# Output stores regrouped: one transfer takes both column halves of a token group, or a whole block of 384 KB, from all 128 partitions

## The chip, the core and the metric

The kernel runs on one core of a Trainium2 chip. TensorE (PE) multiplies, VectorE (DVE), ScalarE (ACT) and GpSimd (POOL) move and convert data, and SyncE (SP) issues nearly all transfers. A transfer is one instruction on SP or ACT; its bytes are moved by the core's 16 DMA engines. On-chip memory has 128 partitions, and a tile is addressed as partitions x elements. The metric is the device time of one execution in microseconds (us), lower is better.

## What is computed

Sigmoid attention, followed by a token-mixing layer on its result. Shapes: q, k and v are (8, 12, 448, 64), the result is (8, 448, 768), all float32.

```python
scores = scale * q @ k.T - log(S)            # per batch and head, S = 448
attn   = 1 / (1 + exp(-scores)) @ v
x      = attn, heads side by side            # (8, 448, 768)
W_tok  = (x @ w_q) @ (x @ w_k).T / sqrt(64)  # (8, 448, 448)
out    = relu(W_tok @ x) @ w_out             # (8, 448, 768)
```

## The kernel before

The work goes by 24 "quads": one batch and four heads each, three quads to a batch. For every quad, q, k and v are loaded (448 KB each) into one of six float32 load buffers (`ld`), cast to bf16, mostly by POOL, transposed, multiplied to scores, passed through the sigmoid on ACT and multiplied with v. When a batch has its three quads, the mixing layer runs for it (`mlp_wqk`, `mlp_wkn`, `mlp_tmp`, `mlp_mix`). When a pair of batches `w` (0 to 3) is done, its last product with `w_out` runs in output chunks, between the matmuls of later quads. The order of all of this is written out by hand as a string of letters (`PLAN`); letter `O` is a step of an output chunk and `D` issues one queued store (`flush(1)`). Instructions stand on each engine in the order in which the program issues them.

There are two kinds of output chunk:

- For the pairs 0 and 1, `out_chunk` makes a block `o` of 128 partitions x 768 columns: 128 tokens of all columns, written in two column halves. A token is `p * 7 + i`, with `p` from 0 to 63 and `i` from 0 to 6 (`NI` = 7), so a block holds two values of `i`, the first on partitions 0 to 63 and the second on 64 to 127. Seven blocks make a pair; in the fourth the two `i` lie in different batches. Its store (L652) is two transfers, one for each half of the partitions, 192 KB each.
- For the pairs 2 and 3, `out_pair` makes a tile of 128 partitions x 2 x 384. Partitions 0 to 63 hold the columns 0 to 383, partitions 64 to 127 the columns 384 to 767; the index in the middle, `y`, tells token index `k` from `k + 4`. Its store (L608) is two transfers of 192 KB, one for each half of the partitions (each column half `x`). There are 12 such tiles, 24 transfers, one of them (the very last) on ACT's queue. The last tiles (`late`) use the load buffers, which are free by then; all others come from a pool of five `o` buffers. The seventh token index is stored apart (L613, L559, L561); the change does not touch that.

`store` is put on a list, and issued at a later `D`, at the latest when an `o` buffer is needed again. The transfers of the SP queue share eight completion semaphores in turn: a transfer is issued only when the eighth before it has landed, and an instruction that waits holds what stands behind it on SP. The loads of the quads are issued on the same queue, between the stores, each as soon as the cast that read the buffer before is done. A transfer's destination and source are access patterns: lists of (step, count), outermost first. The shape that the order shows for a store is that of its destination: `64x768` is 64 token rows of 768 columns, and its source begins with the 64 partitions.

Of the kernel before, what the change touches and what calls it, by code (L numbers as in the profile page):

```python
# [17 lines left out]
def kernel(  # L18
# [12 lines left out]
    nc = tc.nc  # L31
# [5 lines left out]
    NI, NP = 7, 64  # L37
# [4 lines left out]
    HALF = (slice(0, 64), slice(64, 128))  # L42
# [34 lines left out]
    def bank2():  # L77
        n = int(given.pop(0))
        assert not held & {2 * n, 2 * n + 1}
        held.update({2 * n, 2 * n + 1})  # L80
        return n, pairs[n], pairs16[n]

    def bank1():
        b = "abcdefgh".index(given.pop(0))
        assert b not in held
        held.add(b)
        return "abcdefgh"[b], pairs[b // 2][:, b % 2], pairs16[b // 2][:, b % 2]

    def release(fb):
        gone = {2 * fb, 2 * fb + 1} if isinstance(fb, int) else {"abcdefgh".index(fb)}  # L90
        assert gone <= held
        held.difference_update(gone)
# [16 lines left out]
    def ld_next():  # L109
        nld[0] += 1  # L110
        return lds[(nld[0] - 1) % 6]
# [8 lines left out]
    def mm(*args, **kw):  # L120
        products.append(nc.tensor.matmul(*args, **kw))  # L121
# [399 lines left out]
    def flush(n=None):  # L521

        for _, f in stores[:n]:
            f()
        del stores[:n]

    def o_tile(shape):

        while stores and stores[0][0] <= o_tiles[0] - 5:
            flush(1)  # L530
        o_tiles[0] += 1
        return p_o.tile(shape, F32, tag="o", name="o")

    def slot(half, b):

        return b // 2 + (0 if b % 2 == half else NC)

    def middle(w, us, k, part, fb, ps):

        x = part // 2  # L540
        for c in range(part % 2 * NC // 2, (part % 2 + 1) * NC // 2):
            for u in us:
                st = mxs[w].rearrange("p (c u s) -> p c u s", u=2, s=S)[:, c, u, 3 * NP : 4 * NP]
                mm(
                    ps[HALF[u], x, 0:NB], st, wout16[:, c, x * NB : (x + 1) * NB],
                    start=(c == 0), stop=(c == NC - 1),
                )
        if part % 2:
            if not x:
                ot[0] = ld_next()[:, 0:D]  # L550
            o = ot[0][:, x * NB : (x + 1) * NB]
            half = NB // 2
            for y in range(2):
                cols = slice(y * half, (y + 1) * half)
                COPY["vs"[y]](out=o[:, cols], in_=ps[:, x, cols])
            rows = out[2 * w : 2 * w + 2].rearrange("u (p i) d -> (u p) i d", i=NI)[:, NI // 2, x * NB : (x + 1) * NB]
            if x:
                for y in range(2):
                    (nc.sync, nc.scalar)[y].dma_start(out=rows[HALF[y]], in_=o[HALF[y]])  # L559
            else:  # L560
                nc.sync.dma_start(out=rows, in_=o)  # L561
        if part < 3:
            opened.append((w, us, k, part + 1, fb, ps))
        else:
            release(fb)

    def out_pair(act, tail):

        if opened:
            w, us, k, part, fb, ps = opened.pop()  # L570
        else:
            w, us, k = chunks.pop(0)
            part = 0
            fb, ps, _ = bank2()
        if len(us) == 2 and w == MIXED:
            middle(w, us, k, part, fb, ps)
            return
        mx = mxs[w].rearrange("p (b s) -> p b s", b=12)
        at = S // 2 - 32 if len(us) == 2 else k * NP + (32 + S // 2 if us[0] else 0)
        for b in range(3 * part, 3 * part + 3):  # L580
            for y in range(2):
                st = mx[HALF[y], b, at : at + NP]
                if w == MIXED:
                    j = (b - b % 2) * S + us[0] * S + (b % 2) * 4 * NP + k * NP
                    st = mxs[w][HALF[y], j : j + NP]
                for x in range(2):
                    mm(
                        ps[HALF[x], y, 0:NB], st, wout16[HALF[y], slot(y, b), x * NB : (x + 1) * NB],
                        start=(b == 0), stop=(b == 11),
                    )  # L590
        if part < 3:
            opened.append((w, us, k, part + 1, fb, ps))
            return
        late = len(cast) == len(ORDER) + 2
        ends = w == NU // 2 - 1 and us[-1] and len(chunks) < 2
        o = ld_next()[:, 0:D].rearrange("p (b x) -> p b x", b=2) if late else o_tile([P, 2, NB])
        if ends:
            for y in range(2):
                COPY["vs"[y]](out=o[:, y], in_=ps[:, y, 0:NB])
        else:  # L600
            COPY["s" if act else "v"](out=o, in_=ps[:, :, 0:NB])
        release(fb)

        def store():
            for x in range(2):
                cols = slice(x * NB, (x + 1) * NB)
                if len(us) == 1:
                    (nc.scalar if ends and x else nc.sync).dma_start(  # L608
                        out=out[2 * w + us[0]].rearrange("(p i) d -> p i d", i=NI)[:, k : k + 5 : 4, cols], in_=o[HALF[x]],
                    )  # L610
                    continue
                for u in us:
                    nc.sync.dma_start(  # L613
                        out=out[2 * w + u].rearrange("(r n i) d -> i n r d", r=2, i=NI)[NI // 2, :, :, cols],
                        in_=o[64 * x + 32 * u : 64 * x + 32 * u + 32],
                    )

        stores.append((o_tiles[0] - 1, store))
        if tail or late:
            flush()  # L620

    def out_chunk(act, tail):

        if opened:
            w, m, nb, fb, ps = opened.pop()
            part = 1
        else:
            w, m, nb = chunks.pop(0)
            if nb < 0:
                nb = 0  # L630
                chunks.insert(0, (w, m, 1))
            fb, ps, _ = bank1()
            part = 0
        if nb == 0 and not part:
            ot[0] = o_tile([P, D])
        o = ot[0]
        ps = ps if part else ps[:, 0:NB]
        for c in range(part * NC // 2, (part + 1) * NC // 2):
            mm(
                ps, mxs[w][:, 2 * S * c + m * P : 2 * S * c + (m + 1) * P],  # L640
                wout16[:, c, nb * NB : (nb + 1) * NB], start=(c == 0), stop=(c == NC - 1),
            )
        if not part:
            opened.append((w, m, nb, fb, ps))
            return
        COPY["s" if act else "v"](out=o[:, nb * NB : (nb + 1) * NB], in_=ps)  # L646
        release(fb)

        def store():
            for y in range(2):  # L650
                b, i = divmod(2 * m + y, NI)
                nc.sync.dma_start(out=out[2 * w + b].rearrange("(p i) d -> p i d", i=NI)[:, i], in_=o[HALF[y]])  # L652

        if nb:
            stores.append((o_tiles[0] - 1, store))
# [23 lines left out]
    def cols(r):  # L679
        return slice(r.start * HD, r.stop * HD)  # L680
# [8 lines left out]
        out=ident, in_=ident, compare_op=ALU.not_equal, fill=1.0, base=0,  # L689
# [93 lines left out]
    for t16, t32, r, e in (  # L783
# [3 lines left out]
            out=t16[:, r].rearrange("p i b d -> p b i d"),  # L787
            in_=t32[:, :, cols(r)].rearrange("p b (i d) -> p b i d", d=HD),
# [3 lines left out]
    def tr_part(nm, t16, r, e, tiled=False):  # L792
# [19 lines left out]
        out=k016[:, K3].rearrange("p i b d -> p b i d"), in_=k0[:, :, cols(K3)].rearrange("p b (i d) -> p b i d", d=HD),  # L812
# [10 lines left out]
    for t in PLAN:  # L823
# [17 lines left out]
        c = done[kind]  # L841
# [4 lines left out]
        elif kind == "P":  # L846
            n, i = divmod(c, NI)
# [29 lines left out]
        elif kind == "C":  # L877
            for y in range(2):
                nc.sync.dma_start(
                    out=wout16[HALF[y], NC + 2 * c : NC + 2 * c + 2, :], in_=wout16[HALF[1 - y], 2 * c : 2 * c + 2, :],  # L880
# [5 lines left out]
        elif kind == "M":  # L886
            u, x = divmod(c, NC // 2)
# [42 lines left out]
```

## Time and profile before

| | us |
|---|---|
| median of 3 runs (184.32 to 186.18) | 185.74 |
| the profiled execution | 185.85 |
| its span, from the first to the last instruction | 184.1 |
| what lies around the span in that execution | 1.75 |

The page gives the busy time of each engine, the span in 40 slices, the traffic of the DMA queues, the chain of waits that ended last, and the costliest groups of instructions. A group's line has its source line, engine, operation, what it writes and reads, the count, and durations. The share of the DMA engines is a mean over all 16; a share slightly over 1 comes from packets that overlap on an engine. "To landing" is the time from the issue of a transfer until its last completion signal.

### The profile page before, as it was taken

What the parts mean: (1) busy time and instruction counts of PE and PEld (TensorE: products, weight loads), DVE (VectorE), ACT (ScalarE), POOL (GpSimd) and SP (SyncE); (2) the same over time, 40 slices, a digit from 0 to 9 for tenths busy, and PEclk for the clock granted to TensorE, in tenths of its full rate; (3) what the DMA queues carried; (4) which work ended last, traced back from release to release, by engine and by line L of the source; (5) the groups of instructions that cost most, each with busy time, mean ns of one, the idle gap of its engine ahead of it and who ended that gap; (6) DMA issues with size and microseconds to landing.
All of it is one profiled execution on the core that took longest, in us unless ns stands there. A gap on an engine that the chain in (4) does not pass through costs nothing.

```text
span 184.1 us, 8404 instructions
## 1 busy us (share of the span) xinstructions
PE 171.2 (93%) x3618; PEld 112.3 (61%) x3618; DVE 134.0 (73%) x205; ACT 159.9 (87%) x207; POOL 117.0 (64%) x156
## 2 busy tenths in 40 slices
PE   7987778799999999999999999999999999999990
PEld 7544434454564655565656556456778898888970
DVE  2445679988999898988848877689785894694310
ACT  4699998999999999998998999999989979974330
POOL 1445696999799996799999937999999400000000
PEclk9999999999999999999999999999999999999998
DMA  5999999968999768999979998998992343432686
GB/s 176 370 382 283 305 356 333 394 244 267 400 395 390 226 215 272 353 270 366 338 199 309 313 335 271 325 391 286 303 313 65 90 111 90 109 90 66 148 223 172
DMA packets 24261, 48.51 MB, mean 264 GB/s; under 512 B 3872, under 2 KB 16416, under 8 KB 24224
## 3 DMA queue, kind: packets, MB, share of 16 engines
q1 hardware_dynamic: 24000, 47.69, 79.3%
q8 instruction: 28, 0.46, 1.0%
q10 hardware_dynamic: 224, 0.30, 0.6%
q14 instruction: 9, 0.07, 0.1%
HBM read 35.78 MB, written 11.01 MB: 254 GB/s over the span
## 4 chain that ended last, share of the span: by engine, by line
PE 80%; DVE 5%; ACT 5%; issue 3%; POOL 2%; DMA 2%; SPq 0%; ACTq 0%; POOLq 0%
PE banks L121 76%; PE banks L124 4%; ACT at L331 4%; DMA ld<-in_moe_w_k_dram 2%; DVE xt L355 1%; POOL wqk L754 1%; DVE qk L251 1%; POOL qk L211 1%; DVE qk L264 1%; DVE mx L469 1%; POOL v L221 0%; DVE k L221 0%; DVE xn L384 0%; DVE wqk L429 0%; ACT qk L801 0%
## 5 line engine op out<-in xcount | busy, mean ns | idle before, releaser
L331 ACT ACTIVATE at<-banks 128x896 bf16<-128x896 f32 x168 | 141.6, 940 | 6.6 <-PE banks L121 6.1
L121 PE MATMUL banks<-wout,mx 64*64 64x384 bf16 (+2 forms) x816 | 66.2, 324 | 0.7 <-issue 0.6
L121 PE MATMUL banks<-qk 64*64 64x448 bf16 x672 | 60.8, 358 | 4.2 <-ACT at L331 2.7
L121 PEld LDWEIGHTS <-mx 64*64 64x64 bf16 (+2 forms) x816 | 39.5, 105 | 17.5 <-issue 7.1
L211 POOL CAST qk<-ld 128x896 bf16<-128x896 f32 x38 | 44.6, 1193 | 8.4 <-issue 7.2
L121 PE MATMUL banks<-at,v 64*64 64x448 bf16 x672 | 46.7, 350 | 1.5 <-POOL v L221 0.8
L121 PEld LDWEIGHTS <-qk 64*64 64x64 bf16 x672 | 26.6, 105 | 24.8 <-issue 18.0
L355 DVE CAST xt<-banks 128x896 bf16<-128x896 f32 x23 | 25.0, 1086 | 7.6 <-PE banks L121 5.8
L121 PEld LDWEIGHTS <-v 64*64 64x64 bf16 x672 | 23.3, 106 | 7.5 <-issue 1.5
L469 DVE TENSOR_SCALAR mx<-banks 128x896 bf16<-128x896 f32 (+1 forms) x21 | 19.9, 955 | 5.0 <-PE banks L121 4.2
L221 POOL CAST v<-ld 128x896 bf16<-128x896 f32 x22 | 20.3, 930 | 1.2 <-DMA ld<-in_v_dram 0.6
L271 DVE STREAM_TRANSPOSE qk<-qk 128x448 f32<-128x448 f32 x26 | 16.0, 629 | 0.1
L251 DVE STREAM_TRANSPOSE qk<-qk 32x448 f32<-32x448 f32 x24 | 15.3, 636 | 0.6
L384 DVE COPY xn<-banks 128x896 bf16<-128x896 bf16 x21 | 13.1, 624 | 3.6 <-PE banks L124 2.6
L170 POOL COPY qk<-qk 32x448 uint32<-32x448 uint32 x26 | 14.4, 554 | 1.6
L173 POOL COPY qk<-swap 32x448 uint32<-32x448 uint32 x26 | 14.4, 554 | 1.5
L121 PE MATMUL banks<-xt,wqk 64*64 64x448 bf16 (+1 forms) x84 | 13.8, 353 | 0.2 <-ACT at L331 0.2
L646 DVE COPY o<-banks 128x384 f32<-128x384 f32 x17 | 9.4, 553 | 3.4 <-PE banks L121 3.0
L124 PEld LDWEIGHTS <-xt 64*64 64x64 bf16 (+1 forms) x588 | 9.8, 108 | 3.1 <-issue 1.6
L124 PE MATMUL banks<-ident,xt 64*64 64x64 bf16 (+1 forms) x588 | 10.4, 194 | 0.2
L121 PE MATMUL banks<-wqk,tmp 64*64 64x448 bf16 (+3 forms) x72 | 8.7, 291 | 0.0
L121 PE MATMUL banks<-wq,tmp 64*64 64x448 bf16 (+2 forms) x72 | 8.4, 292 | 0.0
(67 smaller groups left out, 136.1 us busy)
## 6 DMA issues: line engine op xcount, KB each, us to landing
ld<-in_q_dram SPq DMA_DIRECT2D x24, 448.0 KB, 6.1
ld<-in_v_dram SPq DMA_DIRECT2D x24, 448.0 KB, 5.9
ld<-in_k_dram SPq DMA_DIRECT2D x23, 448.0 KB, 5.9
out_dram<-o SPq DMA_DIRECT2D x38, 192.0 KB, 4.9
out_dram<-ld SPq DMA_DIRECT2D x14, 192.0 KB, 3.0
ld<-in_moe_w_out_dram SPq DMA_DIRECT2D x6, 384.0 KB, 5.3
wout<-wout SPq DMA_DIRECT2D x6, 192.0 KB, 5.7
out_dram<-o SPq DMA_DIRECT2D x4, 96.0 KB, 1.9
```

Of the source, the lines that this page charges most:

```text
L121: products.append(nc.tensor.matmul(*args, **kw))
L124: products.append(nc.tensor.transpose(*args, **kw))
L170: eng.tensor_copy(out=w[lo, 1], in_=w[hi, 0])
L173: eng.tensor_copy(out=w[hi, 0], in_=z[lo])
L211: COPY[e](out=f[:, :, "qk".index(nm)].rearrange("p e i d y -> p e y i d"), in_=ld.pop((nm, n)).rearrange("p (y i e d) -> p e y i d", y=2, ...
L221: COPY[e](out=t16.rearrange("p i b d -> p b i d"), in_=ld.pop((nm, n)).rearrange("p b (i d) -> p b i d", i=NI),)
L251: nc.vector.transpose(out=qk[n][other : other + 32, h].rearrange("p t i n -> p (t i n)").bitcast(F32), in_=w[own : own + 32, 1 - h],)
L271: nc.vector.transpose(out=qk[n][:, t].rearrange("p t i n -> p (t i n)").bitcast(F32), in_=w)
L331: nc.scalar.activation(dst, src, ACTF.Sigmoid, bias=attn_bias, scale=attn_scale)
L355: COPY[eng](out=xt(u, j), in_=ps)
L384: COPY[eng](out=xn, in_=ps)
L469: nc.vector.tensor_scalar(dst, ps, moe_scale, 0.0, ALU.mult, ALU.max)
```

## The change

The two `store` functions address their transfers in another way. The number of bytes, the tiles, the arithmetic and the places at which `store` is called stay as they are.

- In `out_pair` there are still two transfers of 192 KB to a tile, but each takes one `y` (one token index) from all 128 partitions, with both column halves. The destination is written as column half, token, column: counts 2, 64, 384.
- In `out_chunk` one transfer of 384 KB takes the whole block of 128 partitions. The destination is token index, token, column: counts 2, 64, 768. The fourth block of each pair, whose two token indices lie in different batches, keeps its two transfers.

```diff
         def store():
+            if len(us) == 1:
+                for y in range(2):
+                    (nc.scalar if ends and y else nc.sync).dma_start(
+                        out=out[2 * w + us[0]].rearrange("(p i) (x c) -> i x p c", i=NI, x=2)[k + 4 * y], in_=o[:, y],
+                    )
+                return
             for x in range(2):
                 cols = slice(x * NB, (x + 1) * NB)
-                if len(us) == 1:
-                    (nc.scalar if ends and x else nc.sync).dma_start(
-                        out=out[2 * w + us[0]].rearrange("(p i) d -> p i d", i=NI)[:, k : k + 5 : 4, cols], in_=o[HALF[x]],
-                    )
-                    continue
                 for u in us:
...
         def store():
+            b, i = divmod(2 * m, NI)
+            if i + 1 < NI:
+                nc.sync.dma_start(out=out[2 * w + b].rearrange("(p i) d -> i p d", i=NI)[i : i + 2], in_=o)
+                return
             for y in range(2):
                 b, i = divmod(2 * m + y, NI)
                 nc.sync.dma_start(out=out[2 * w + b].rearrange("(p i) d -> p i d", i=NI)[:, i], in_=o[HALF[y]])
```

On SP, in the middle of the program, block stores of the pair 0 stand between the loads of later quads. `ld_100` to `ld_105` are the six load buffers; a row's shape is that of its destination.

```order
-L652 DMA out_dram<-o 64x768 x2
+L653 DMA out_dram<-o 2x64x768
 L189 DMA ld_102<-in_q_dram 128x896
 L197 DMA ld_103<-in_v_dram 128x2x448
 L197 DMA ld_104<-in_v_dram 128x2x448
-L652 DMA out_dram<-o 64x768 x6
+L653 DMA out_dram<-o 2x64x768 x3
 L197 DMA ld_105<-in_v_dram 128x2x448
 L189 DMA ld_100<-in_k_dram 128x896
 L189 DMA ld_101<-in_k_dram 128x896
-L652 DMA out_dram<-o 64x768 x2
+L653 DMA out_dram<-o 2x64x768
```

Two transfers became one at each place, and no load changed its place. The outermost count of the destination was 64 and is 2; that of the source was 64 partitions and is 128.

On SP, at the end of the program, the last tiles are stored. Before:

```order
L608 DMA out_dram<-ld_105 64x2x384 x2
L608 DMA out_dram<-ld_100 64x2x384 x2
L608 DMA out_dram<-ld_101 64x2x384
L561 DMA out_dram<-ld_102 128x384
L559 DMA out_dram<-ld_102 64x384
```

And in the changed program:

```order
L607 DMA out_dram<-ld_105 2x64x384 x2
L607 DMA out_dram<-ld_100 2x64x384 x2
L607 DMA out_dram<-ld_101 2x64x384
L561 DMA out_dram<-ld_102 128x384
L559 DMA out_dram<-ld_102 64x384
```

Number and place are the same; the outermost count of the destination went from 64 to 2 here too. On the other engines nothing moved.

## The prediction

> **What bounds the kernel now.** I read the page first: the busy times, the slices, the traffic and the chain of waits.
>
> ```profile
> span 184.1 us, 8404 instructions
> PE 171.2 (93%) x3618; PEld 112.3 (61%) x3618; DVE 134.0 (73%) x205; ACT 159.9 (87%) x207; POOL 117.0 (64%) x156
> DMA  5999999968999768999979998998992343432686
> DMA packets 24261, 48.51 MB, mean 264 GB/s; under 512 B 3872, under 2 KB 16416, under 8 KB 24224
> PE 80%; DVE 5%; ACT 5%; issue 3%; POOL 2%; DMA 2%; SPq 0%; ACTq 0%; POOLq 0%
> ```
>
> PE holds 80% of the chain, transfers 2%. But the DMA digits stand at 9 for three quarters of the span: the 16 engines have little room, and what slows one of them is felt. Then the stretches (columns: window and length, busy us of PE, PEld, DVE, ACT, POOL, the granted clock, the DMA share, GB/s):
>
> ```profile
> 46.50:50.50 4.00, 4.00 (x69) 2.36 (x70) 3.85 (x8) 4.00 (x7) 3.15 (x4) 1.00 1.04 404
> 70.00:135.00 65.00, 65.00 (x1188) 38.39 (x1188) 52.96 (x80) 62.22 (x82) 54.78 (x73) 1.00 0.94 311
> 106.60:108.40 1.80, 1.80 (x36) 0.86 (x32) 1.17 (x2) 1.80 (x4) 0.82 (x2) 1.00 1.00 373
> 161.00:178.00 17.00, 16.64 (x480) 15.11 (x472) 8.28 (x17) 8.32 (x16) 0.00 (x0) 1.00 0.51 122
> 176.00:180.00 4.00, 3.66 (x64) 2.49 (x56) 1.21 (x3) 1.32 (x3) 0.00 (x0) 1.00 0.92 225
> 181.00:182.00 1.00, 0.00 (x0) 0.00 (x0) 0.00 (x0) 0.00 (x0) 0.00 (x0) 1.00 0.88 280
> ```
>
> From 70 to 135 us, where the block stores run between the loads, PE is busy 65.00 of 65.00 us and the DMA engines 0.94 of the time. A full queue moves 404 GB/s (46.5 to 50.5), that is 404/16 = 25.3 GB/s for one engine.
>
> All transfers of the program, by the list of issues (count, KB each, median us to landing):
>
> ```profile
> ld<-in_q_dram SPq DMA_DIRECT2D x24, 448.0 KB, 6.1
> ld<-in_v_dram SPq DMA_DIRECT2D x24, 448.0 KB, 5.9
> ld<-in_k_dram SPq DMA_DIRECT2D x23, 448.0 KB, 5.9
> out_dram<-o SPq DMA_DIRECT2D x38, 192.0 KB, 4.9
> out_dram<-ld SPq DMA_DIRECT2D x14, 192.0 KB, 3.0
> ld<-in_moe_w_out_dram SPq DMA_DIRECT2D x6, 384.0 KB, 5.3
> wout<-wout SPq DMA_DIRECT2D x6, 192.0 KB, 5.7
> out_dram<-o SPq DMA_DIRECT2D x4, 96.0 KB, 1.9
> ld<-in_k_dram SPq DMA_DIRECT2D x1, 256.0 KB, 4.2
> ld<-in_k_dram SPq DMA_DIRECT2D x1, 192.0 KB, 3.3
> ld<-in_moe_w_q_dram SPq DMA_DIRECT2D x1, 192.0 KB, 3.8
> ld<-in_moe_w_k_dram SPq DMA_DIRECT2D x1, 192.0 KB, 5.1
> out_dram<-ld ACTq DMA_DIRECT2D x1, 192.0 KB, 3.8
> out_dram<-ld SPq DMA_DIRECT2D x1, 96.0 KB, 2.6
> out_dram<-ld ACTq DMA_DIRECT2D x1, 96.0 KB, 2.7
> ```
>
> The counts add up to 146. The page has 3872 packets under 512 B. The two loads of w_q and w_k move rows of 64 floats, 256 B: 2 x 192 KB / 256 B = 1536 packets. The other 2336 are 146 x 16: every transfer ends with 16 small packets. I read them as one completion from each of 16 engines, so before the change each transfer is dealt over all 16.
>
> **The change, step by step.** What decides is over how many engines a store is dealt. In the program before, every destination and source begins with a count of 128, 64 or 32, as the shapes of the order show, and 16 goes into each of them. The changed stores begin with 128 on the source side and with 2 on the destination side. If the dealing goes by the outermost counts, which the rows before cannot show but never contradict, a share must be a whole part of both, and 2 shares are the most: two engines carry the store, each 64 rows, and 14 carry nothing. I take this as the likeliest case.
>
> The Trainium skill, "DMA: Bandwidth & Descriptors", section "Why a DMA increments its semaphore by 16 and not by 1", states it as a rule: the engine count is the largest number up to 16 that divides the slowest dimension above 1 of both patterns, and on SP's and ACT's queues the lowest-numbered engines are taken. The trace agrees as far as its 146 x 16 packets go; no run here has a count below 16. By that rule the sum is the one below, with the same two engines each time.
>
> The work of one of these two engines, from the first changed store on. The counts of the loads behind it, and of the stores:
>
> ```profile
> L189 SPq DMA_DIRECT2D ld<-in_k_dram x9: 327/333/1437, 76.3 to 127.4; - x9
> L189 SPq DMA_DIRECT2D ld<-in_q_dram x9: 328/333/1087, 77.3 to 129.4; - x9
> L197 SPq DMA_DIRECT2D ld<-in_v_dram x10: 378/382/1023, 81.2 to 128.2; - x10
> L652 SPq DMA_DIRECT2D out_dram<-o x28: 467/588/1382, 70.0 to 133.9; - x28
> DMA to landing us min/median/max: 4.6/4.9/5.5
> ```
>
> (The last line is of the first six L652 stores alone.)
>
> - Blocks: 28 stores were 14 blocks; 12 become one transfer of 393,216 B, half of it on each engine: 12 x 196,608 = 2.36 MB. At 25.3 GB/s one takes 7.8 us, where two half stores took 2 x 192 KB at 404 GB/s = 1.0 us.
> - Tiles: 24 transfers of 196,608 B, half each: 24 x 98,304 = 2.36 MB; 3.9 us for one, before 0.5.
> - What is dealt over 16 as before: 28 loads x 28,672 B = 0.80 MB; two blocks left as four stores x 12,288 B = 0.05; six wout copies x 12,288 = 0.07; the small stores, 4 x 6,144 and 24,576 = 0.05. Together 0.97 MB.
>
> The sum is 5.69 MB, at 25.3 GB/s 225 us. It begins where the queue ahead of the first block store is done: issued at 70.0, landed up to 5.5 us later, less its own 0.5: 75.0. All of it follows in the engine's order, so the last store lands at 75 + 225 = 300 us. Before, the last one (issued at 180.4, landed 2.6 later, 183.0) left 1.1 us to the end of the span. Span: 301. Around it lie 185.85 - 184.1 = 1.75 us, so 303 us, against a profiled 185.85 and a median of 185.74.
>
> Does this engine ever run empty? That would lengthen the sum. Up to the last load (129.4) it carries loads that the program issues as soon as a buffer is free, and up to 23 us of blocks ahead of them (x3 in the order). A load dealt over 16 lands only with its slowest share, so POOL's casts, and PE behind them, wait. Behind the last load stand 3 x 7.8 + 24 x 3.9 = 117 us of stores, while the kernel before needed 184.1 - 129.4 = 55 us from that issue to its end. So computation gets ahead, waits for `o` and load buffers that stores have yet to leave, and keeps the queue full. SP waits for the eighth transfer before; the loads queued behind that wait are late, but eight transfers in flight keep the engine fed. I add nothing.
>
> SP has 12 transfers fewer, 12 x 0.588 = 7.1 us of issuing; SPq is 0% of the chain, so it is worth nothing. What the change ends, two engines at a time reading one half of the partitions, shows in stores at 225/0.92/16 = 15.3 GB/s per busy engine (176 to 180); this goes in any case, and is inside the rate.
>
> The rate is the unknown. No row shows a store on two engines. At the slow end stands the one late store from 128 partitions, alone on the queue at 181 to 182 us: 280/0.88/16 = 19.9 GB/s, or 286 us, end 364. A stretch of block stores in a full queue (106.6 to 108.4) has 373/16 = 23.3: 244 us, end 322. At the quick end no row goes above 25.3, but there all 16 share what lies behind them; if two alone ran 10% faster: 205 us, end 283. I take 25.3, as these two queues are never empty.
>
> **Rivals.** *The stores stay dealt over 16 engines* (by tokens, or by the source's 128 partitions). For it: bytes and packets stay the same, and 16 goes into 64 and 128. Against: the destination's outermost count is 2. This case ends on the other side, not slower. It decides if the count of 2 is merged away or passed over. Then the price is what waits for these stores: PE has no gap from 70 to 135; in the chain SPq has 0%; among those who waited for stores stands a single line.
>
> ```profile
>   ACT ld L555: 1.1, 1
> ```
>
> So 0 to 1.1 us come out: 184.7 to 185.9. The Trainium skill, same page, "Rules for kernel authors", says that two transfers to disjoint partition halves gain nothing and one of 128 partitions is to be used; no run here shows that yet, and by it this case would be the one.
>
> *Two engines, but other ones each time.* Then the work is even in sum, and no engine collects 225 us. A load behind a group of blocks still waits up to 7.8 - 1.0 = 6.8 us for its slowest share. On SP five groups of blocks stand ahead of loads, 5 x 6.8: 0 to 34 us, less what the buffers cover; the last store adds 3.9 - 0.5 = 3.4. That gives 189 to 223 us; I take 197, since six load buffers lie ahead of the casts. Against it: nothing in a full queue asks for turns, and the transfers before needed none.
>
> **How the numbers follow.** Two fixed engines: 0.84. Dealt over 16: 0.10. Changing pairs: 0.04. Something else, slower: 0.02. The likeliest gives 303 us. From its rates come 283 to 364; I open the lower end to 280. About one part in twenty of the first case may lie outside, so that the range holds 0.8. The other cases are left out of it. Within 1% (1.9 us) is about what a measurement of this kernel can tell from no change. The 16-engine case gives at most 0.6%, so it counts as the same, 0.07, and 0.03 of it as faster, should freed transfers help somewhere that the chain does not show. Slower: 0.84 + 0.04 + 0.02 = 0.90.
>
> **What would show it.** Packets under 512 B: 1536 + 98 x 16 + 36 x 2 = 3176 if the 36 changed transfers have two completions each; 1536 + 134 x 16 = 3680 if they have 16. The DMA digits of the last 80 us at 1 (two of 16 engines), with 2 x 25.3 = 51 GB/s. PE's slices with gaps from 80 us on, and its busy time near 171 as before. Chain: DMA in the first place, with stores. SP's waits for landings, which are small now, in tens of us. A transfer count right and a rate wrong would show as 3176 packets with another GB/s at the end. The forecast falls altogether if the small packets are 3680, or if PE stays at 93%.

## The result: 304.68 us, and the profile after

| | before | changed |
|---|---|---|
| median of 6 runs, us | 186.38 (184.32 to 187.05) | 304.68 (303.27 to 304.78) |
| ratio | | 1.635, 95% interval 1.627 to 1.644 |
| span of the profiled execution, us | 184.1 | 302.9 |
| packets under 512 B | 3872 | 3176 |

The page of the changed kernel: the busy times, three rows of the 40 slices (each now 7.6 us), the traffic, and the chain of waits by engine and by line.

```profile
span 302.9 us, 8385 instructions
PE 187.1 (62%) x3618; PEld 118.8 (39%) x3618; DVE 133.9 (44%) x205; ACT 161.4 (53%) x207; POOL 117.3 (39%) x156
PE   8878899999994079908588596686699400000000
DMA  7989979976328698113394931111131111111111
GB/s 234 388 253 388 388 228 375 355 250 202 98 95 261 215 271 283 54 52 118 147 274 142 316 115 54 54 54 50 52 101 54 50 50 50 50 50 50 62 72 48
DMA packets 23565, 48.51 MB, mean 160 GB/s; under 512 B 3176, under 2 KB 15720, under 8 KB 23528
DMA 47%; PE 22%; ACT 9%; SPq 3%; DVE 3%; POOL 3%; issue 2%; DVEq 0%; ACTq 0%; POOLq 0%
DMA out_dram<-o 30%; PE banks L121 21%; DMA out_dram<-ld 10%; ACT at L331 8%; DMA ld<-in_k_dram 6%; SPq L607 3%; PE banks L124 2%; POOL qk L211 2%; DVE o L601 1%; DVE mx L469 1%; POOL qk L173 0%; POOL qk L170 0%; DVE qk L271 0%; DVE xt L355 0%; POOL v L221 0%
```

Read it from the right. In the last eight slices PE does nothing; the DMA digit is 1, and the traffic 48 to 72 GB/s, mostly 50. The chain went from 80% PE to 47% DMA, two kinds of stores ahead of all loads. The bytes are the same, 48.51 MB. The small packets are 1536 + 98 x 16 + 36 x 2 = 3176, to the packet, as it must be if each of the 36 changed transfers ends with two completions, where all others have 16. One of the 36 can be seen nearly by itself. ACT's queue (`q10`) carries just two transfers, a changed one and the store of 96 KB, in 192 packets of data. Its packets (count, MB, share of the engines), before and changed:

```profile
q10 hardware_dynamic: 224, 0.30, 0.6%
q10 hardware_dynamic: 210, 0.29, 0.3%
```

That is 192 + 16 + 16 before, and 192 + 16 + 2 now.

Four windows of the changed kernel in which its stores stand nearly alone on the queue (the last two columns are the DMA share and GB/s):

```profile
75.50:78.00 2.50, 2.50 (x46) 1.53 (x44) 2.38 (x5) 2.44 (x4) 1.16 (x3) 1.00 0.13 53
180.00:210.00 30.00, 20.69 (x438) 16.23 (x434) 11.88 (x16) 16.40 (x20) 9.09 (x14) 0.85 0.14 53
240.00:285.00 45.00, 0.00 (x0) 0.00 (x0) 1.27 (x3) 1.02 (x3) 0.00 (x0) 0.52 0.14 52
255.00:268.00 13.00, 0.00 (x0) 0.00 (x0) 0.71 (x2) 0.00 (x0) 0.00 (x0) 0.50 0.13 50
```

In the first, two changed blocks are under way. The second still holds the ends of some loads, and the third the small store on ACT's queue, issued at 280.6 us and dealt over all 16. In the last there are the changed stores alone: a share of 0.13 over 16 engines is 2.1 engines, two that are always busy, and 50 GB/s over two is 25 GB/s each. Before, one of 16 engines in a full queue moved 404/16 = 25.3. So an engine works as fast as ever; 14 are left out.

How this reaches PE is seen where loads stand behind the first blocks. POOL of the changed kernel, 84 to 101 us, in order of time (start, length, what; in brackets the idle time ahead and what ended it):

```profile
84.14 0.93 POOL L221 CAST v<-ld 128x896 bf16<-128x896 f32 x1
100.97 2.26 POOL L211 CAST qk<-ld 128x896 bf16<-128x896 f32 x2 [15.90 <-DMA ld<-in_k_dram]
```

The load of k is dealt over 16 engines, but two of its shares stand behind three blocks, 3 x 7.8 us on those engines, the first of which begins at 75 us. It lands when they do; POOL waits 15.9 us for it, and PE's slices of 91 to 106 us show 4 and 0. Some of the large waits, over the whole changed kernel (engine and line, waited for whom, us in total, times, longest):

```profile
ACT at L331 <- PE banks L121: 53.2, 33, 13.0
POOL v L221 <- DMA ld<-in_v_dram: 26.9, 5, 21.8
DVE o L601 <- DMA out_dram<-o: 17.8, 5, 6.4
POOL qk L211 <- DMA ld<-in_k_dram: 16.6, 3, 15.9
DVE o L647 <- DMA out_dram<-o: 13.7, 3, 7.6
```

Late loads and output buffers that have not been emptied hold up computation. Even so it is done long before the stores: the window 240 to 285 has no matmul at all.

### The profile page after: what moved, and what is told of

It is laid out like the page before. It is cut to its first block, busy times and chain, and to the rows that moved or that the text cites. A ratio compares the mean times of both kernels' runs of the same rounds, so it can differ in the third digit from the quotient of the medians.

```text
span 302.9 us, 8385 instructions
## 1 busy us (share of the span) xinstructions
PE 187.1 (62%) x3618; PEld 118.8 (39%) x3618; DVE 133.9 (44%) x205; ACT 161.4 (53%) x207; POOL 117.3 (39%) x156
## 2 busy tenths in 40 slices
DMA packets 23565, 48.51 MB, mean 160 GB/s; under 512 B 3176, under 2 KB 15720, under 8 KB 23528
## 4 chain that ended last, share of the span: by engine, by line
DMA 47%; PE 22%; ACT 9%; SPq 3%; DVE 3%; POOL 3%; issue 2%; DVEq 0%; ACTq 0%; POOLq 0%
DMA out_dram<-o 30%; PE banks L121 21%; DMA out_dram<-ld 10%; ACT at L331 8%; DMA ld<-in_k_dram 6%; SPq L607 3%; PE banks L124 2%; POOL qk L211 2%; DVE o L601 1%; DVE mx L469 1%; POOL qk L173 0%; POOL qk L170 0%; DVE qk L271 0%; DVE xt L355 0%; POOL v L221 0%
## 5 line engine op out<-in xcount | busy, mean ns | idle before, releaser
L121 PE MATMUL banks<-qk 64*64 64x448 bf16 x672 | 65.1, 380 | 37.6 <-DVE xt L355 13.6
L121 PE MATMUL banks<-wout,mx 64*64 64x384 bf16 (+2 forms) x816 | 72.8, 356 | 7.5 <-DVE xt L355 4.0
L121 PEld LDWEIGHTS <-mx 64*64 64x64 bf16 (+2 forms) x816 | 42.0, 114 | 28.5 <-issue 17.1
L121 PEld LDWEIGHTS <-qk 64*64 64x64 bf16 x672 | 27.4, 110 | 61.8 <-issue 54.7
L121 PE MATMUL banks<-at,v 64*64 64x448 bf16 x672 | 49.5, 365 | 0.6 <-ACT at L331 0.3
L121 PEld LDWEIGHTS <-v 64*64 64x64 bf16 x672 | 24.5, 111 | 7.2 <-issue 1.3
L271 DVE STREAM_TRANSPOSE qk<-qk 128x448 f32<-128x448 f32 x26 | 16.0, 630 | 22.4 <-POOL qk L173 22.3
L251 DVE STREAM_TRANSPOSE qk<-qk 32x448 f32<-32x448 f32 x24 | 15.3, 636 | 0.6
L601 DVE COPY o<-banks 128x768 f32<-128x768 f32 x6 | 5.7, 957 | 18.1 <-DMA out_dram<-o 17.8
L124 PEld LDWEIGHTS <-xt 64*64 64x64 bf16 (+1 forms) x588 | 10.5, 112 | 3.3 <-issue 1.8
L647 ACT COPY o<-banks 128x384 f32<-128x384 f32 x11 | 5.4, 491 | 10.1 <-DMA out_dram<-o 9.5
```

The costliest lines, as they stand in the source:

```text
L124: products.append(nc.tensor.transpose(*args, **kw))
L251: nc.vector.transpose(out=qk[n][other : other + 32, h].rearrange("p t i n -> p (t i n)").bitcast(F32), in_=w[own : own + 32, 1 - h],)
L271: nc.vector.transpose(out=qk[n][:, t].rearrange("p t i n -> p (t i n)").bitcast(F32), in_=w)
```

## The experiments

The theory is that of the prediction: a transfer is dealt by the outermost counts of its two patterns, so a count of 2 leaves two engines, and the price is what these two have to move one after the other. Its rivals say that the price lies in the store itself: in reading 128 partitions, in the size of 384 KB, or in the two places of memory to which one store goes.

**even16: the same stores, to 128 rows in one even step.** Two batches of a pair lie 64 x 7 tokens apart, so that row `p` of both forms one run of 128 rows, 7 tokens from one to the next.

```diff
-                        out=out[2 * w + us[0]].rearrange("(p i) (x c) -> i x p c", i=NI, x=2)[k + 4 * y], in_=o[:, y],
+                        out=out[2 * w : 2 * w + 2].rearrange("u (p i) (x c) -> (u p) i x c", i=NI, x=2)[:, k + 4 * y, us[0]], in_=o[:, y],
...
-                nc.sync.dma_start(out=out[2 * w + b].rearrange("(p i) d -> i p d", i=NI)[i : i + 2], in_=o)
+                nc.sync.dma_start(out=out[2 * w : 2 * w + 2].rearrange("u (p i) d -> (u p) i d", i=NI)[:, m], in_=o)
```

> Same transfers as the changed kernel, from all 128 partitions and of the same sizes, but each store goes to 128 output rows of one even step (token rows of two batches), so that its destination begins with a count of 128, not 2. Which rows of the output a block lands in is changed; all bytes are stored once. Dealing by the outermost counts: 16 engines again, 3680 packets under 512 B, 184.5 to 187 us, no slower than before; at most 1.1 us is gained. If one large store from 128 partitions, or the merging, were what costs: it stays near 300 us.

Measured: 185.28 us (median of 12), beside a before of 186.22; ratio 0.996, interval 0.993 to 0.999. The stores read 128 partitions, the blocks are 384 KB, and nothing is lost. The rivals of size and of partitions fall.

**rows2, rows4, rows8: the same rows in 2, 4 and 8 runs.** To both destinations of even16 a split of the 128 rows is added, for rows4:

```diff
-...[:, k + 4 * y, us[0]], in_=o[:, y],
+...[:, k + 4 * y, us[0]].rearrange("(n h) c -> h n c", h=4), in_=o[:, y],
...
-...[:, m], in_=o)
+...[:, m].rearrange("(n h) d -> h n d", h=4), in_=o)
```

Each run has every fourth row.

> The same 128 rows as in even16, but written as 2 runs of 64 (every second row), so that the destination begins with a count of 2; the rows within a block are permuted. Dealing by the outermost counts: two engines, 3176 small packets, 300 to 307 us, as the changed kernel. If where the rows lie in memory (the two token indices, the two column halves) were what costs, it is as fast as even16.

> As rows2 with 4 runs of 32: the destination begins with 4. Dealing by the outermost counts: four engines, 1536 + 98 x 16 + 36 x 4 = 3248 small packets. Each of the four then has 2.36 + 0.97 = 3.33 MB behind 75 us, 132 us at 25.3 GB/s: 75 + 132 + 2.9 = 210 us if it never runs empty, less where computation is the bound; I expect 200 to 212. If a first count below 16 always meant the same slow path, it is near 300; if it cost nothing of its own, 186.

> As rows2 with 8 runs of 16: the destination begins with 8. Dealing by the outermost counts: eight engines, 3392 small packets; 1.18 + 0.97 = 2.15 MB on each of them, 85 us, so their queue would be done at 160 us and no longer sets the end: 185 to 190 us. A cost for each changed store that does not fall with the engine count would show as more.

Measured, one execution each: 304.59, 214.38 and 190.59 us. The traffic line of their pages, of even16, rows2, rows4 and rows8 in turn:

```profile
DMA packets 24069, 48.51 MB, mean 265 GB/s; under 512 B 3680, under 2 KB 16224, under 8 KB 24032
```

```profile
DMA packets 23565, 48.51 MB, mean 160 GB/s; under 512 B 3176, under 2 KB 15720, under 8 KB 23528
```

```profile
DMA packets 23637, 48.51 MB, mean 228 GB/s; under 512 B 3248, under 2 KB 15792, under 8 KB 23600
```

```profile
DMA packets 23781, 48.51 MB, mean 257 GB/s; under 512 B 3392, under 2 KB 15936, under 8 KB 23744
```

All four counts are those expected: 16, 2, 4 and 8 completions for each of the 36 stores. (On ACT's queue, with its one changed store, the packets are 224, 210, 212 and 216.) The output rows within a block's set are the same in all four, in another order, so the place in memory is not the cause either. rows2 repeats the median of the changed kernel within 0.1 us. rows4 is 2 us above the range that I gave, at four engines, and rows8 half a microsecond above its own. Two windows of rows4, from 190 us to 210 us, nearly without matmuls, and from 75 to 135 us:

```profile
190.00:210.00 20.00, 1.10 (x14) 0.53 (x10) 0.71 (x2) 0.54 (x2) 0.00 (x0) 0.66 0.32 115
75.00:135.00 60.00, 51.49 (x816) 28.12 (x815) 38.94 (x59) 48.14 (x64) 38.12 (x50) 0.94 0.78 244
```

At the end the stores set the time, 0.32 x 16 = 5.1 engines' worth of share for four engines and the last small stores. In the middle PE is busy 51.5 of 60.0 us. I had bounded the time by the four engines' queue alone (210 us); it came out 4 us later. Counted in the trace's packets, fewer than four are in flight for only 0.5 us between 75 and 210 us, so no empty queue is seen. The first packet of a changed block starts at 74.1 us and the last of all ends at 211.3: 3.33 MB in 137 us is 24.3 GB/s for one engine, where I had taken 25.3, and that is about the 4 us. rows8 is 4.4 us above its before, 186.22; its page shows one wait of 3.1 us for a store (ACT, L601), and the rest stays open.

**blocks_only and pairs_only: half of the change each.** The one keeps `out_chunk`'s new store and has `out_pair`'s old one, the other the reverse. Against the changed kernel:

```diff
# blocks_only: out_pair as before
-            if len(us) == 1:
-                for y in range(2):
...
# pairs_only: out_chunk as before
-            b, i = divmod(2 * m, NI)
-            if i + 1 < NI:
...
```

> Only the whole-block stores of out_chunk are changed (12 transfers of 384 KB); out_pair's stores are as before. Two engines for these 12: 2.36 MB on each beside the loads of the time from 70 to 135 us, so casts and PE wait for loads that land late. A queue account from the issue times of before gives some 42 us of delay to computation, and the tail of stores dealt over 16 hides nothing: 222 to 238 us. 3872 - 12 x 16 - 12 x 14 = 3512 small packets. If the blocks cost nothing because loads are ahead: 186.

> Only out_pair's stores are changed (24 transfers of 192 KB); whole blocks are stored as before. All but a few of their loads are done by then, so nothing is late but the stores: 24 x 3.9 = 93 us behind the first one, whose queue is free at 139 us: 139 + 93 + 2.9 = 235 us, 228 to 240. 3872 - 24 x 14 = 3536 small packets. PE's last work stays behind by the buffers that stores free late.

Measured: 238.84 and 237.86 us, beside a before of 186.56. The excesses, 52 and 51 us, add up to 104; the whole change costs 304.68 - 186.38 = 118. That the whole costs more than its halves fits a queue in which the tiles' stores stand behind blocks that are themselves late; no run tests it. pairs_only came out 2.9 us above the 235 computed, within its range: there no load is behind the stores, and the sum is only the queue. The page's slices of pairs_only, PE and DMA:

```profile
PE   7987889999999999999999999999993000000000
DMA  6989997999579999999997921151111111111120
```

PE runs full until its end, as before, and nine slices of 5.9 us follow with stores on two engines. blocks_only was just above its range. Its queue is not the end; its loads are late, and when PE was starved its granted clock went down. The window 75 to 180 us of blocks_only (the clock is the third number from the right):

```profile
75.00:180.00 105.00, 73.35 (x1188) 42.77 (x1190) 50.53 (x78) 61.03 (x79) 53.01 (x71) 0.84 0.55 176
```

And the window of the kernel before in which it does as many matmuls, from 75 us on too:

```profile
75.00:138.50 63.50, 63.27 (x1188) 38.10 (x1183) 51.31 (x78) 60.26 (x80) 54.77 (x74) 1.00 0.94 309
```

The 1188 matmuls are busy 10 us longer in blocks_only. My account had no term for these 10 us, which are about what is missing between its middle, 230, and 238.84; no run shows the clock's part by itself.

**half2: half-partition stores, with a count of 2.** The kernel before, its 28 block stores as they are, from 64 partitions and 192 KB each; only the 64 rows are written in two runs of 32.

```diff
-                nc.sync.dma_start(out=out[2 * w + b].rearrange("(p i) d -> p i d", i=NI)[:, i], in_=o[HALF[y]])
+                nc.sync.dma_start(out=out[2 * w + b].rearrange("(n h i) d -> i h n d", h=2, i=NI)[i], in_=o[HALF[y]])
```

> The kernel before, with its half-partition block stores (28 transfers of 192 KB from 64 partitions), but the 64 rows of each written as 2 runs of 32, so that the destination begins with 2; the rows within a half are permuted. No store reads 128 partitions and none is merged. Dealing by the outermost counts: two engines for these 28, 28 x 98,304 B = 2.75 MB on each: like blocks_only and a little more, 225 to 245 us; 3872 - 28 x 14 = 3480 small packets. If reading 128 partitions or the size of 384 KB were what costs: 186 us.

Measured: 251.60 us, 3480 packets under 512 B, so two completions each. No store reads 128 partitions, none is merged, and it is 12.8 us slower even than blocks_only. On each of the two engines it has 2.75 - 2.36 - 0.05 MB = 0.34 MB more, which at 25 GB/s are 14 us (an estimate that takes all else to be alike). My range ended at 245 because it was built on the range of blocks_only, which was too low; PE is busy 184.7 us here and 184.8 us there, against 171.2 before.

**even16_pairs and own_buffer: where do 0.4% come from?** even16 was faster than before by 0.1 to 0.7%. The one has even16's stores in `out_pair` alone; the other is the kernel before with

```diff
-                ot[0] = ld_next()[:, 0:D]
+                ot[0] = o_tile([P, D])
```

> As even16, but only out_pair's 24 stores read all 128 partitions (128 even output rows each, blocks permuted); the whole blocks are stored as before. If the 0.4% of even16 comes from the last tiles, where its PE is 0.6 us ahead from 168 us on: 0.3 to 0.5% faster than before again, about 185.3 us. If it comes from the merged block stores (12 instructions less on SP): no difference, 186.2 us.

> The kernel before with one line changed: the last middle tile (L550) is written into an `o` buffer that is long free, not into the load buffer of an earlier tile whose store has to land first. If ACT's 1.1 us before L555 are a wait for that store, they go, and up to 1.1 us of the time: 0.3 to 0.6% faster. If it waits for DVE's copy into the same tile (as even16's profile puts it, with the same 1.1 us): no difference, 186.2 us.

Measured: even16_pairs 184.51 us, ratio 0.993 (0.990 to 0.997); own_buffer 186.75 us, ratio 1.004 (1.001 to 1.007). So the tiles' stores alone bring the gain, a little more of it than expected, and the merged blocks are not needed for it. ACT's 1.1 us before L555 were not a wait for a store. own_buffer came out slower by 0.1 to 0.7%, which neither of its two cases had; why stays open. ACT's waits near the end, before and own_buffer:

```profile
ACT ld L555 <- DMA out_dram<-ld: 1.1, 1, 1.1
```

```profile
ACT o L555 <- DVE o L555: 1.7, 2, 1.1
```

With a buffer that no store holds, the same 1.1 us stand there and are put down to DVE, which writes the other half of the tile first. What the tiles' stores gain is visible in them: the issue lists give 3.0 us to landing before, and 2.1 us for even16 and even16_pairs. The window of 176 to 180 us, in which the kernel before moved 15.3 GB/s per busy engine from halves of the partitions, reads in even16:

```profile
176.00:180.00 4.00, 2.90 (x46) 1.73 (x36) 1.27 (x3) 1.11 (x3) 0.00 (x0) 1.00 0.79 283
```

That is 283/0.79/16 = 22.4 GB/s. How this reaches PE is open: in the profiles PE's last matmul is 0.8 us earlier in even16 and 1.7 us in even16_pairs, but where it gains them no wait names a store, and the runs of the kernel before that the ratio rests on differ among themselves by 2.6 us. A version with the right rows would need tiles whose 128 rows lie in one even step, hence another order of the chunks; it wasn't tried.

## Why the prediction was right

303 us was forecast for the likeliest case, 304.68 was measured. By its steps:

- **Two engines for each changed store.** The deciding step, argued from shapes alone, held: 3176 packets, and with rows2, rows4, rows8 and even16 the completions follow the first count of the destination: 2, 4 and 8, and 16 for a count of 128. The rule of the Trainium skill ("DMA: Bandwidth & Descriptors", section "Why a DMA increments its semaphore by 16 and not by 1"), the largest number up to 16 that divides both counts, agrees with all of them; since all counts tried are powers of two, the runs do not tell it from a plain minimum.
- **The same two engines each time.** The profile does not name a packet's engine. But the first two changed blocks were both issued by 72.2 us, and while both are under way, from 75.5 to 78 us, the share is 0.13, two engines' worth. Changing pairs would have had four engines busy there. The rival of changing pairs is out.
- **The rate.** 25.3 GB/s from a queue on 16 engines was taken for two; 25 was measured. That two engines alone might run faster, for which the range was opened by 10%, did not happen, and the 19.9 GB/s of a lone store was far too low.
- **The sum.** 5.69 MB from 75 us on gave a span of 301; it is 302.9. The parts fit as well as the total, so the closeness is not two errors that cancel: in the trace's packets the first of a changed block starts at 75.2 us (75.0 computed) and the last of all ends at 301.6 (300 computed), and between them, until 299 us, fewer than two are in flight for only 0.3 us. So the two engines were not seen empty, as the sum had assumed. That computation would be ahead of the stores held too: no matmul after 240 us.
- **The rival on the other side**, stores dealt over 16, was wrong for this change but right in its price: given 128 rows in one step, even16 takes 185.28 us where 184.7 to 185.9 stood in the prediction. Its reason, though, ACT's 1.1 us, fell with own_buffer.
- **Not as predicted:** PE's busy time is 187.1 us, not 171, since its granted clock fell when it had no work. SP's waits for landings of stores are 9.6 us ahead of loads and 7.0 us at the end, not tens of us; it is held in the issuing itself (below).
- **A misreading that cost nothing.** The DMA digits of the kernel before stand at 9 in 21 of the 40 slices, not in three quarters of them. The sum rests on the stretch from 70 to 135 us, where the share of 0.94 is read rightly.

The Trainium skill, "DMA: Bandwidth & Descriptors", section "Rules for kernel authors", asks for one transfer of 128 partitions in place of two of half the partitions. even16 follows it with a count of 128 on both sides and gains 0.4%, though by even16_pairs (0.7%) it is the tiles' stores from 128 partitions, still two to a tile, that bring this; the changed kernel follows it with a count of 2 and takes 1.635 times as long.

## What to carry to other kernels

When a store is merged, look at the outermost count of its patterns (the runs here vary the destination's alone), not only at the number of partitions and bytes: one count of 2 in front of 64 rows took 14 of 16 engines away, and the loads behind it paid as well. A count of completions is in the page (small packets, less the ones that the data explain), and tells after one run how widely transfers are dealt. To price such a fault, add up what the busiest engine has to move from there on; that came within 1%, and no wait of the profile before would have shown it.

## What had not been expected

**SP is held while it issues.** In the kernel before an L608 issue took 0.6 us; the same stores are L607 in the changed one (SP's own instructions, duration in ns min/median/max, first and last start in us):

```profile
L608 SPq DMA_DIRECT2D out_dram<-ld x13: 595/596/1358, 161.1 to 178.2; - x13
L607 SPq DMA_DIRECT2D out_dram<-ld x13: 3224/3810/6620, 235.2 to 285.6; - x13
L653 SPq DMA_DIRECT2D out_dram<-o x12: 521/902/10192, 70.9 to 179.4; - x12
```

The median of 3.81 us for a store of the tail is about the time that two engines need to move it, 196,608 B / 50 GB/s = 3.9 us. I read it as an issue that does not end until there is room behind the transfers ahead, which no run tests; the loads that stand behind it on SP are held for as long.

**PE's granted clock falls when it is starved.** The rows of the two pages, before and changed:

```profile
PEclk9999999999999999999999999999999999999998
PEclk9999999999999569975979799597799955555555
```

It falls to between 5 and 7 in slices with a gap of PE or right behind one, and stands at 5 in the eight slices at the end, in which PE does nothing. The mean of the score matmuls, by the groups of the two pages, rose from 358 to 380 ns. Late loads cost twice: the wait, and slower matmuls after it.
